# Eight memory recalls of a fused attention and GLU kernel: one float32 product each, replaced by three products of split operands

## The chip, the cores and the metric

The kernel runs on one core of one Trainium2 chip. The metric is the device time of one execution in microseconds (us); lower is better. Before the change the median of three runs is 689.55 us (689.37 to 689.55).

## The reference, cut to what matters

One layer with a residual: a layernorm, then two branches that both read it, and their sum.

```python
xn = layernorm(x)                        # 2048 tokens x 448
return x + A(xn) + B(xn)
# B: (sigmoid(xn @ w_gate) * (xn @ w_up)) @ w_down,   1792 hidden columns
# A: 16 heads of 28, the tokens in N = 4 blocks of L = 512, each block with causal attention of its own
M = z = 0
for s in range(N):
    a_dot = softmax(qs @ ks.T * scale + mask) @ vs
    pq = phi(qs)                         # t + 1 if t > 0 else exp(t)
    a_mem = (pq @ M) / (pq @ z + 1e-6)   # the recall: what earlier blocks left in the memory
    outs.append(g * a_mem + (1 - g) * a_dot)
    pk = phi(ks)
    M = M + pk.T @ vs;  z = z + pk.sum(tokens)
```

The line that the change touches is `pq @ M`, for the blocks s = 1, 2 (block 0 recalls an empty memory, and block 3 stays as it was).

## The kernel before

Most products run in float32r (f32r), which keeps fewer bits than float32. To keep float32 precision the kernel splits an operand in two f32r parts: a high part (a copy, ScalarE, line 85 or 436) and a low part (the operand minus its high part, VectorE or GpSimd, lines 86 and 437), and sums high x high, high x low and low x high in PSUM.

The program has a front and a long second stage. The front (lines 276 to 577) makes values, keys and queries of the four blocks of 512 tokens and keeps the memory; the second stage interleaves the GLU with the attention of the heads and ends with the output projection. The order of TensorE, ScalarE and VectorE in the front is the order in which the Python code is written; that of GpSimd is chosen by the scheduler. In each block b of the front:

- four times `values(b, t)`: 11 products of 128 x 448 (tile `pv`), and a copy on ScalarE that stores them in `vst`;
- between them, for b > 1, the recalls of block b - 1. A recall covers four heads (one of NG = 4 groups): it multiplies the group's memory `mst` (112 x 128, the four heads' blocks on a diagonal) with the features `phi` (112 x 512) that a DMA brought back from DRAM (`fd`). Recall i stands one call of `values` behind the one of its own number; recall 3 stands behind the first product of the next part;
- behind the product (tile `n`) VectorE transposes (line 402), divides and gates in `weigh` (lines 132, 133, 136), transposes back (line 404, tile `tb`), and GpSimd issues a DMA to `od` (line 405);
- seven times `keys_queries(b, c)`: 11 products of 128 x 512 (tile `pp`), whose split result goes to DRAM, and behind them the transposes of keys, `update(b, i)`, which adds to the memory (lines 389 and 390: VectorE, `dm` and `mst`), and `turn`, which transposes the next block's normalised tokens `xn` (tile `pt`, line 95).

In block 2, between the values, VectorE also takes the statistics of block 3's tokens (lines 294 to 296, ending in `vh`), and ScalarE takes their root `y` (line 301). That root stands in ScalarE's order in front of the copy of the second `values`. Block 3 has no statistics; in its place the split of a GLU weight, `wgu` (lines 85 and 86), stands there.

The 4k buffers (`four_k`, four of them) are shared by the split keys and queries and, from the change on, by what it adds.

Of the kernel before, what the change touches and what calls it, by code (L numbers as in the profile page):

```python
# [9 lines left out]
F32 = mybir.dt.float32  # L10
F32R = mybir.dt.float32r
AF = mybir.ActivationFunctionType
# [4 lines left out]
P = 128  # L17
# [10 lines left out]
NG = H // HG  # L28
GW = HG * DH
# [32 lines left out]
def kernel(  # L62
# [11 lines left out]
    V, A, G, T = nc.vector, nc.scalar, nc.gpsimd, nc.tensor  # L74
# [40 lines left out]
    def bank(name, tag):  # L115
        return ps.tile([P, L], F32, name=name, tag=tag, bufs=banks[tag])
# [10 lines left out]
    def weigh(pool, num, g, add):  # L127

        r = pool.tile([P, 16], F32, name="rc", bufs=2)
        n3 = num.rearrange("p (m c) -> p m c", c=32)  # L130
        if add:
            V.tensor_scalar_add(r, n3[:, :, DH], add)
            V.reciprocal(r, r)
        else:
            V.reciprocal(r, n3[:, :, DH])
        V.scalar_tensor_tensor(n3[:, :, :DH], n3[:, :, :DH], g, r.unsqueeze(2).to_broadcast([P, 16, DH]),
                               op0=ALU.mult, op1=ALU.mult)
# [11 lines left out]
    def four_k(dtype, name):  # L149
        return mid.tile([P, 2, L], dtype, name=name, tag="4k", bufs=4)  # L150
# [125 lines left out]
    with tc.tile_pool(name="front", bufs=2) as sb, tc.manual_schedule(engines=FRONT):  # L276
# [4 lines left out]
        wv = [late_pair("wv") for _ in range(4)]  # L281
        wv = [wv[c // 2][:, c % 2, :] for c in range(8)]
        wqk = [sb.tile([P, 8, P], F32R, name=f"wqk{c}", bufs=1) for c in range(7)]
        mst = [[sb.tile([GW, P], F32, name=f"mst{n}_{i}", bufs=1) for i in range(NG)] for n in range(2)]
        one = sb.tile([P, 1], F32, name="one", bufs=1)
        kn = eight_k(F32, "kn").rearrange("p (t a) n -> p t (a n)", t=NT)

        def statistics(b, t0, steps):

            stats = sb.tile([P, steps, 6], F32, name=f"stats{steps}")  # L290
            mv = sb.tile([P, steps, 2], F32, name=f"mv{steps}")
            vh = sb.tile([P, steps], F32, name=f"vh{steps}")
            for t in range(steps):
                V.bn_stats(stats[:, t, :], acc[b][:, t0 + t, :])
                V.bn_aggr(mv[:, t, :], stats[:, t, :])
            V.tensor_scalar(vh, mv[:, :, 1], EPS, -0.5, op0=ALU.add, op1=ALU.mult)
            return mv, vh

        def root(vh):
            y = sb.tile([P, vh.shape[1]], F32, name=f"y{vh.shape[1]}")  # L300
            A.activation(y, vh, AF.Sqrt, scale=-2.0)
            return y

        def rstd(mv, vh, y):

            steps = vh.shape[1]
            tm = sb.tile([P, steps], F32, name=f"tm{steps}")
            V.reciprocal(y, y)
            if steps == 1:
                V.tensor_scalar(tm, y, y, vh, op0=ALU.mult, op1=ALU.mult)  # L310
                V.tensor_scalar(y, tm, 1.5, y, op0=ALU.add, op1=ALU.mult)
            else:
                V.tensor_mul(tm, y, y)
                V.tensor_mul(tm, tm, vh)
                V.scalar_tensor_tensor(y, tm, 1.5, y, op0=ALU.add, op1=ALU.mult)
            return [(mv[:, t, 0:1], y[:, t:t + 1]) for t in range(steps)]

        def normalise(b, t, mean, y):
            xn = sb.tile([P, 512], F32, name="xn")
            V.tensor_scalar(xn[:, :D].rearrange("p (m h c) -> p h m c", h=H, c=4),  # L320
                              acc[b][:, t, :].rearrange("p (h m c) -> p h m c", h=H, c=4), mean, y,
                              op0=ALU.subtract, op1=ALU.mult)
            if b == 0:
                A.activation(xn[:, D:], xn[:, 384:D], AF.Copy)
            else:
                G.tensor_copy(xn[:, D:], xn[:, 384:D])
            return xn
# [15 lines left out]
        def values(b, t):  # L343
            pv = bank("pv", "p")
            value_terms(b, t, pv, EARLY[1] if b == 0 else TERMS)
            store_values(b, t, pv)
# [45 lines left out]
        def phi_queries(b, i):  # L392
            phi = sb.tile([GW, L], F32, name="phi", tag="e", bufs=5)
            nc.sync.dma_start(phi, fd[b][i * GW:(i + 1) * GW])
            return phi

        def recall(b, i, phi):
            ts = sb.tile([P, L], F32, name="ts", bufs=1)
            tb = sb.tile([P, L], F32, name="tb", bufs=2)
            n2 = bank("n2", ("m", "pd")[i % 2])  # L400
            T.matmul(n2, mst[b % 2][i], phi, start=True, stop=True)  # L401
            V.transpose(ts, n2)
            weigh(sb, ts, gate[:, i:i + 1], MEM_EPS)
            V.transpose(tb, ts)
            nc.gpsimd.dma_start(od[b][P * i:P * (i + 1)], tb)
# [28 lines left out]
        def split_qk(c):  # L434
            r = raw_qk[c].rearrange("p (c n) -> p c n", c=4)
            A.activation(wqk[c][:, 0:4, :], r, AF.Copy)
            G.tensor_sub(wqk[c][:, 4:8, :], r, wqk[c][:, 0:4, :].bitcast(F32))
# [66 lines left out]
        for b in range(NB):  # L504
            last = b == NB - 1
            phi, xn = {}, {}
            if b > 1:
                phi = {i: phi_queries(b - 1, i) for i in range(NG)}
            st = None
            for t in range(3 if b == 0 else 0, NT):  # L510
                values(b, t)
                if b > 1 and t > 0:
                    recall(b - 1, t - 1, phi[t - 1])
                if b == 0:
                    split_qk(t)
                if last:
                    continue
                if t == (3 if b == 0 else 0):
                    mv, vh = statistics(b + 1, 0, NT)
                if t == (3 if b == 0 else 0):  # L520
                    st = mv, vh, root(vh)
                if t == (3 if b == 0 else 2):
                    A.activation(one, ident[:, 0:1], AF.Exp)
            if st and b > 0:
                st = rstd(*st)
                for n in range(2):
                    xn[n] = normalise(b + 1, n, *st[n])
            e = {}
            for k, c in enumerate((3, 4, 5, 6, 0, 1, 2) if last else range(7)):
                e[c] = keys_queries(b, c)  # L530
                if b == 0 and c + 4 < 7:
                    split_qk(c + 4)
                if k == 0:
                    if b > 1:
                        recall(b - 1, NG - 1, phi[NG - 1])
                    if b == 0:
                        st = rstd(*st)
                    if b == 0:
                        A.activation(gate, gate, AF.Exp, scale=-1.0)
                        V.tensor_scalar_add(gate, gate, 1.0)  # L540
                        V.reciprocal(gate, gate)
                        V.tensor_scalar(gate_n, gate, -1.0, 1.0, op0=ALU.mult, op1=ALU.add)
                if (b, k) in ((0, 3), (1, 0)):
                    with tc.issue_after(stored[b, c]):
                        nc.sync.dma_start(acc[b + 2], x_block(b + 2))
                if (b, k) in ((2, 1), (3, 0)):
                    with tc.issue_after(stored[b, c]):
                        next(ffn)
                if last:
                    if k > 0:  # L550
                        next(ffn)
                    if 2 <= k < 6:
                        phi[k - 2] = phi_queries(b, k - 2)
                    if k > 4:
                        begin[k - 5]()
                        recall(b, k - 5, phi[k - 5])
                    continue
                if 2 <= k < 6:
                    key_rows(k - 2, e[k - 2])
                if 4 <= k:  # L560
                    update(b, k - 4)
                if k == 6:
                    update(b, 3)
                n = k - 1 if b == 0 else k + 1
                if 2 <= n < 6:
                    turn(b + 1, n - 2, xn[n - 2])
                if 0 <= n < 4 and n not in xn:
                    xn[n] = normalise(b + 1, n, *st[n])
                if b == 2 and k == 6:
                    next(ffn)  # L570
            if last:
                for i in range(2):
                    for _ in range(FILLS[i]):
                        next(ffn)
                    if i == 0:
                        begin[2]()
                    recall(b, i + 2, phi[i + 2])
# [3 lines left out]
    sb = ctx.enter_context(tc.tile_pool(name="att", bufs=1, reuse_waits="tile"))  # L581
# [252 lines left out]
```

## Time and profile before

| | before |
|---|---|
| median of three runs | 689.55 us |
| the profiled execution's own time | 689.46 us |
| its span in the trace | 687.7 us |
| granted clock of TensorE | 0.999 |
| TensorE / VectorE / ScalarE / GpSimd busy | 99% / 83% / 50% / 22% |
| products of recalls (line 401) | 24 instructions for 12 recalls, from 82.3 to 156.7 us |

The span is what the profiler recorded from the first to the last instruction; 1.76 us lie outside it. A row of a timeline has the start, the duration, the engine, the line, the operation, what it writes and reads, how many instructions are merged in it, and in brackets the idle time before it with what ended it. A row of the chain of waits has the start, the duration, the engine, the tile and the line. PE is TensorE, DVE VectorE, ACT ScalarE, POOL GpSimd. Types are printed as f32 in most rows whether the operand is float32 or f32r.

### The profile page before, as it was taken

The page shows a single profiled execution, that of the slowest core. Times are in us where ns is not written, and L with a number is a line of the kernel's source. Part 1 is how long each engine was busy: PE and PEld are TensorE (multiplying, and loading weights), DVE is VectorE, ACT ScalarE, POOL GpSimd, SP SyncE. Part 2 cuts the span into 40 slices and gives each one's busy share as a digit, 9 for nine tenths or more (in the row PEclk, how much of TensorE's full clock was granted, in tenths as well). Part 3 has the DMA queues.
Part 4 walks back from the last instruction along what each step waited for, and adds up shares of the span by engine and source line. Part 5 has one row for each costly group of instructions (what it writes and reads, how often), then busy time and mean ns, then how long its engine had stood idle before and what let it go on. Part 6 is the DMA issues. An engine that isn't in the chain of part 4 may idle for free.

```text
span 687.7 us, 10438 instructions
## 1 busy us (share of the span) xinstructions
PE 681.7 (99%) x3594; PEld 566.6 (82%) x3594; DVE 567.4 (83%) x994; ACT 342.6 (50%) x563; POOL 151.3 (22%) x349
## 2 busy tenths in 40 slices
PE   8999999999999999999999999999999999999997
PEld 7898888778878787787878878787787878878897
DVE  6765795767788988998898989989898899889863
ACT  4837555343554555543655446454653565446320
POOL 3500020101223222232332222322322322222000
PEclk9999999999999999999999999999999999999999
DMA  7446556696233323243223252314333332423342
GB/s 267 181 150 238 198 214 242 249 330 174 71 94 92 80 86 86 56 128 112 56 64 107 57 141 56 109 47 116 82 94 77 96 71 64 95 79 95 95 153 106
DMA packets 45796, 84.37 MB, mean 123 GB/s; under 512 B 6320, under 2 KB 20400, under 8 KB 45232
## 3 DMA queue, kind: packets, MB, share of 16 engines
q1 hardware_dynamic: 42736, 76.37, 35.8%
q0 software_dynamic: 3008, 7.34, 4.9%
q8 instruction: 28, 0.46, 0.3%
q14 instruction: 24, 0.20, 0.1%
HBM read 51.05 MB, written 32.64 MB: 122 GB/s over the span
## 4 chain that ended last, share of the span: by engine, by line
PE 70%; DVE 14%; issue 9%; POOL 4%; DMA 1%; ACT 1%; SPq 0%; POOLq 0%; ACTq 0%
PE pgu L247 26%; PE pd L173 13%; PE pp L355 10%; PE po L771 5%; PE pv L335 5%; PE st L612 3%; PE pa L687 3%; DVE mx L629 3%; DVE w L666 2%; POOL w L627 2%; DVE acc L174 2%; PE pmm L383 2%; PE n L401 2%; DVE hh L259 1%; DVE mx L633 1%
## 5 line engine op out<-in xcount | busy, mean ns | idle before, releaser
L247 PE MATMUL pgu<-xs,wgu 128*128 128x512 f32 x1232 | 304.1, 394 | 0.0
L247 PEld LDWEIGHTS pgu<-xs,wgu 128*128 128x128 f32 x1232 | 228.2, 188 | 47.4 <-issue 2.2
L173 PE MATMUL pd<-wdn,hh 128*128 128x448 f32 x672 | 156.0, 367 | 0.0
L627 POOL TENSOR_SCALAR_AFFINE_SELECT w<-w 128x256 f32<-128x256 f32 (+1 forms) x160 | 81.2, 509 | 236.4 <-ACT w L616 183.6
L173 PEld LDWEIGHTS pd<-wdn,hh 128*128 128x128 f32 x672 | 122.5, 188 | 12.3 <-issue 0.6
L667 ACT ACTIVATE w<-w 128x1024 f32<-128x1024 f32 (+1 forms) x96 | 87.3, 915 | 65.0 <-DVE w L666 64.2
L666 DVE TENSOR_TENSOR w<-w,mb 128x1024 f32<-128x1024 f32 (+1 forms) x96 | 98.9, 1045 | 0.1
L616 ACT ACTIVATE w<-st 128x512 f32<-128x512 f32 x128 | 74.9, 590 | 45.3 <-PE st L612 44.9
L629 DVE TRANSPOSE_TENSOR_REDUCE mx<-w 128x32 f32<-128x1024 f32 x64 | 79.0, 1235 | 17.0 <-POOL w L627 17.0
L355 PE MATMUL pp<-xs,wqk 128*128 128x512 f32 x308 | 77.7, 401 | 0.0
L174 DVE TENSOR_TENSOR acc<-pd,acc 128x448 f32<-128x448 f32 x112 | 67.1, 599 | 1.2 <-PE pd L173 1.1
L355 PEld LDWEIGHTS pp<-xs,wqk 128*128 128x128 f32 x308 | 56.8, 188 | 13.4 <-issue 2.4
L258 ACT ACTIVATE hh<-sg 128x512 fp32r<-128x512 f32 x56 | 35.2, 628 | 56.4 <-DVE sg L256 49.3
L612 PE MATMUL st<-qk 84*128 84x128 f32 (+3 forms) x256 | 61.9, 312 | 0.0
L255 ACT ACTIVATE sg<-pgu 128x512 f32<-128x512 f32 x56 | 33.2, 594 | 49.4 <-PE pgu L247 49.2
L612 PEld LDWEIGHTS st<-qk 84*128 84x128 f32 x256 | 47.6, 189 | 6.9 <-ACT w L616 0.3
L656 DVE STREAM_TRANSPOSE mb<-top 128x1024 f32<-128x1024 f32 x32 | 39.8, 1242 | 10.5 <-POOL top L653 10.1
L362 DVE TENSOR_TENSOR qk<-pp,qk 128x512 fp32r<-128x512 f32 x28 | 19.3, 688 | 29.8 <-ACT e L360 23.7
L259 DVE SCALAR_TENSOR_TENSOR hh<-sg,hh 128x512 fp32r<-128x512 f32 x56 | 38.7, 691 | 2.6 <-ACT hh L258 2.4
L335 PE MATMUL pv<-wv,xs 128*128 128x448 f32 x176 | 39.6, 376 | 0.4 <-DVE xs L102 0.3
L687 PE MATMUL pa<-w,vv 128*32 128x128 f32 (+3 forms) x512 | 39.7, 436 | 0.2
L256 DVE SCALAR_TENSOR_TENSOR sg<-sg,pgu 128x512 f32<-128x512 f32 x56 | 37.3, 665 | 1.8 <-PE pgu L247 1.6
(100 smaller groups left out, 640.6 us busy)
## 6 DMA issues: line engine op xcount, KB each, us to landing
qk<-qd SPq DMA_DIRECT2D x192, 112.0 KB
qd<-qk SPq DMA_DIRECT2D x28, 512.0 KB
raw<-in_w_ffn SPq DMA_DIRECT2D x14, 512.0 KB
vd<-vst SPq DMA_DIRECT2D x4, 1024.0 KB
vv<-vd SPq DMA_DIRECT2D x16, 256.0 KB
od<-w POOLq DMA_DIRECT2D x16, 256.0 KB, 3.8
sums<-od SPq DMA_DIRECT2D x32, 128.0 KB
out<-acc SPq DMA_DIRECT2D x16, 224.0 KB
```

What stands on the lines that cost most here:

```text
L173: T.matmul(pd[:, :D], l, r, start=n == 0, stop=n == len(mms) - 1)
L174: V.tensor_add(acc[b][:, t, :], pd[:, :D], acc[b][:, t, :])
L247: T.matmul(dst, wgu[f][:, w, side * P:(side + 1) * P], xs[b][:, a, :], start=n == 0, stop=n == len(TERMS) - 1)
L335: T.matmul(pv[:, :D], xs[b][:, a, t * P:(t + 1) * P], wv[w], start=n == 0, stop=n == len(TERMS) - 1)
L355: T.matmul(pp, wqk[c][:, w, :], xs[b][:, a, :], start=n == 0, stop=n == len(TERMS) - 1)
L612: T.matmul(st[:, at:at + L - kb * P], self.qk[:KS, 1, h, kb * P:(kb + 1) * P], self.qk[:KS, 0, h, kb * P:], start=True, stop=True)
L616: A.activation(w, st, AF.Copy)
L627: G.affine_select(d, d, pattern=pattern, base=0, channel_multiplier=-1, compare_op=ALU.is_ge, fill=MASK)
L629: V.tensor_reduce(mx[:, 16 * (n - 1):16 * (n + 1)], w3[:, n // 2, :2 * L].rearrange("p (b n) -> p b n", n=32), axis=mybir.AxisListType.X, ...
L666: V.tensor_sub(w, w, m)
L667: A.activation(w, w, AF.Exp, scale=SCALE)
L687: T.matmul(pa[32 * j:32 * j + 32, kb * P:], self.vv[:, kb, 32 * j:32 * j + 32], self.pairs[j // 2].block(j % 2, kb), start=kb == 0, stop=k ...
```

## The change

The eight recalls of blocks 1 and 2 (which run in blocks 2 and 3 of the front) become three f32r products each. The four memories of a block lie in one tile, so that one copy and one subtraction split all four (`memory_parts`, at the start of the block). Each recall's features are split by `parts`: for the first recall at the start of the block, for recall t between `values(b, t)` and recall t - 1. The high parts are copied on ScalarE, the low parts subtracted on GpSimd. The four recalls at the end of the front still are float32 products.

```diff
-        mst = [[sb.tile([GW, P], F32, name=f"mst{n}_{i}", bufs=1) for i in range(NG)] for n in range(2)]
+        memory = [sb.tile([GW, NG, P], F32, name=f"mst{n}", bufs=1) for n in range(2)]
+        mst = [[m[:, i, :] for i in range(NG)] for m in memory]
...
+        def memory_parts(b):
+
+            m = four_k(F32R, "ms")[:GW].rearrange("p a (i n) -> p a i n", i=NG)
+            A.activation(m[:, 0], memory[b % 2], AF.Copy)
+            G.tensor_sub(m[:, 1], memory[b % 2], m[:, 0].bitcast(F32))
+            return m
+
+        def parts(i, phi, m):
+
+            f = four_k(F32R, "phis")[:GW]
+            A.activation(f[:, 0, :], phi, AF.Copy)
+            G.tensor_sub(f[:, 1, :], phi, f[:, 0, :].bitcast(F32))
+            return [(m[:, a, i, :], f[:, w, :]) for a, w in ((0, 0), (0, 1), (1, 0))]
+
...
-            T.matmul(n2, mst[b % 2][i], phi, start=True, stop=True)
+            terms = phi if isinstance(phi, list) else [(mst[b % 2][i], phi)]
+            for n, (l, r) in enumerate(terms):
+                T.matmul(n2, l, r, start=n == 0, stop=n == len(terms) - 1)
...
                 phi = {i: phi_queries(b - 1, i) for i in range(NG)}
+                mp = memory_parts(b - 1)
+                phi[0] = parts(0, phi[0], mp)
...
                 if b > 1 and t > 0:
+                    phi[t] = parts(t, phi[t], mp)
                     recall(b - 1, t - 1, phi[t - 1])
```

ScalarE at the start of block 2, before: the last exponential of block 1's features (`e`), the copies of the values (`vst`) and the root `y` between the first and the second.

```order
L361 ACTIVATE e<-e 128x512
L339 ACTIVATE vst<-pv 128x16x28
L301 ACT_TABLE_LOAD
L301 ACTIVATE y_936<-vh_926 128x4
L339 ACTIVATE vst<-pv 128x16x28 x2
```

The same place now:

```order
L362 ACTIVATE e<-e 128x512
L401 ACTIVATE ms<-mst_123 112x512
L408 ACTIVATE phis<-phi 112x512
L340 ACTIVATE vst<-pv 128x16x28
L302 ACT_TABLE_LOAD
L302 ACTIVATE y_936<-vh_926 128x4
L340 ACTIVATE vst<-pv 128x16x28
L408 ACTIVATE phis<-phi 112x512
L340 ACTIVATE vst<-pv 128x16x28
L408 ACTIVATE phis<-phi 112x512
```

The copies of the memory (`ms`) and of the first features stand ahead of the first `vst`; the copy of the second recall's features stands behind the root and behind the second `vst`.

GpSimd in block 2 before: nothing but the DMAs of the recalls' results and the copies of a strip of `xn`.

```order
L326 COPY xn<-xn 128x64 x7
L405 DMA od_92<-tb 128x512 x3
L326 COPY xn<-xn 128x64 x2
L405 DMA od_92<-tb 128x512
L326 COPY xn<-xn 128x64 x2
```

GpSimd in block 2 now:

```order
L327 COPY xn<-xn 128x64 x7
L402 TENSOR_TENSOR ms<-mst_123,ms 112x512
L409 TENSOR_TENSOR phis<-phi,phis 112x512 x2
L422 DMA od_92<-tb 128x512
L409 TENSOR_TENSOR phis<-phi,phis 112x512
L422 DMA od_92<-tb 128x512
```

Three subtractions stand ahead of the first DMA; that of the third recall's features stands behind the DMA of the first recall's result, and that of the fourth behind the DMA of the second. VectorE's and the DMA queue's orders are the same as before.

## The prediction

> **What bounds the kernel now.** I read the page first, then the chain of waits in the stretch where the recalls run, then the timelines of that stretch.
>
> ```profile
> PE 681.7 (99%) x3594; PEld 566.6 (82%) x3594; DVE 567.4 (83%) x994; ACT 342.6 (50%) x563; POOL 151.3 (22%) x349
> ```
>
> A busy share of 99% is an average over stages, so the stage decides. The chain of waits through block 2 of the front:
>
> ```profile
> 78.06 4.42 PE pv L335 x22
> 82.48 0.86 PE n L401 x2
> 83.34 2.21 PE pv L335 x11
> 85.55 0.86 PE n L401 x2
> 86.41 2.21 PE pv L335 x11
> 88.61 0.86 PE n L401 x2
> 89.47 2.51 PE pp L355 x11
> 91.99 0.86 PE n L401 x2
> 92.85 2.52 PE pp L355 x11
> 95.37 0.44 PE pt L95 x4
> ...
> 119.42 0.86 PE n L401 x2
> ```
>
> Each piece begins where the one before ends: TensorE sets the pace here without a gap, so TensorE time saved in a recall is time saved, and any wait put into TensorE's order is time lost. Both pass in full to what follows, since TensorE works through its order strictly in sequence.
>
> **What is removed.** A float32 recall costs 0.86 us on the chain. An f32r product of the same 512 columns costs 2.51 / 11 = 0.228 us (the pp piece), so three cost 0.685. Each recall gains 0.175 us, eight gain 1.40 us. That is the whole gain; the transposes, gates and DMAs behind a recall stay.
>
> **What is added, and on whose time.** Two times five copies on ScalarE and two times five subtractions on GpSimd. The nearest rows are the split of a query weight in the first block, which has the same 512 columns:
>
> ```profile
> L437 POOL TENSOR_TENSOR wqk<-stage,wqk 128x512 fp32r<-128x512 f32 x4 | 5.1, 1293 | 4.8 <-ACT wqk L436 4.8
> ...
> L436 ACT ACTIVATE wqk<-stage 128x512 fp32r<-128x512 f32 x4 | 2.4, 621 | 0.0
> ```
>
> I take 1.29 us for a subtraction and 0.62 for a copy: 12.9 us more on GpSimd and 6.2 on ScalarE, neither on the chain by itself. In such a row the busy time and the mean of one in ns stand behind the first bar.
>
> Here a rule can be held against the row. The Trainium skill, GPSIMD Engine Reference, section 3.1 (Elementwise), gives a two-input GpSimd operation about 2.6 cycles an element; at the 1.2 GHz that it uses, an estimate by that page is 1.11 us for 512 columns. With it the three subtractions ahead of the second recall would be done 0.55 us sooner, and the sum below would end near +1.4 instead of +2.0 us. The row was measured in this kernel, and it decides.
>
> **What GpSimd's subtractions do to VectorE.** This is the step on which the forecast rests. First the rows:
>
> ```profile
> 18.95 3.79 POOL L437 TENSOR_TENSOR wqk<-stage,wqk 128x512 fp32r<-128x512 f32 x3 [1.10 <-ACT wqk L436]
> 19.11 0.59 DVE L294 BATCH_NORM_STATS2 stats<-acc 128x6 f32<-128x448 f32 x1
> ...
> 25.55 1.30 POOL L437 TENSOR_TENSOR wqk<-wqk_raw,wqk 128x512 fp32r<-128x512 f32 x1 [2.81 <-ACT wqk L436]
> 25.80 1.08 DVE L313 TENSOR_TENSOR tm<-y 128x4 f32<-128x4 f32 x1
> 26.91 0.16 DVE L314 TENSOR_TENSOR tm<-tm,vh 128x4 f32<-128x4 f32 x1
> ...
> 486.99 1.21 DVE L86 TENSOR_TENSOR wgu<-raw,wgu 128x1024 fp32r<-128x1024 f32 x1
> 487.12 1.75 POOL L652 COPY top<-top 32x32 f32<-32x32 f32 x1 [0.28 <-DVE top L651]
> 488.12 0.67 DVE L259 SCALAR_TENSOR_TENSOR hh<-sg,hh 128x512 fp32r<-128x512 f32 x1
> ```
>
> While GpSimd subtracts, VectorE's statistics (one input from SBUF) take their usual 0.59 us. But the 128x4 product at 25.80, with two inputs from SBUF, takes 1.08 us where its like a moment later takes 0.16, and it ends at 26.88, just behind the subtraction's end at 26.85: it was held until GpSimd was done. The other way round a tiny GpSimd copy at 487.12 lasts 1.75 us, until two back-to-back VectorE operations of that kind are over (488.79). So I read: a VectorE operation with two SBUF inputs and a GpSimd operation exclude each other; whichever is second waits for the end of the first.
>
> **Block 2, step by step.** The rows of the place where the new work lands:
>
> ```profile
> 75.51 0.46 SPq L394 DMA_DIRECT2D phi<-fd  x1
> 77.47 0.63 ACT L361 ACTIVATE e<-e 128x512 f32<-128x512 f32 x1
> 79.06 0.29 DVE L390 TENSOR_TENSOR mst<-mst,dm 112x128 f32<-112x128 f32 x1
> 79.58 0.29 DVE L390 TENSOR_TENSOR mst<-mst,dm 112x128 f32<-112x128 f32 x1
> 79.79 0.62 DVE L294 BATCH_NORM_STATS2 stats<-acc 128x6 f32<-128x448 f32 x1
> 82.85 0.17 DVE L296 TENSOR_SCALAR vh<-mv 128x4 f32<-128x4 f32 x1
> 83.05 0.20 ACT L301 ACTIVATE y<-vh 128x4 f32<-128x4 f32 x1 [0.89 <-DVE vh L296]
> 83.16 0.53 ACT L339 ACTIVATE vst<-pv 128x448 f32<-128x448 f32 x1
> 83.38 0.72 DVE L402 STREAM_TRANSPOSE ts<-n 128x512 f32<-128x512 f32 x1 [0.36 <-PE n L401]
> 84.63 0.68 DVE L136 SCALAR_TENSOR_TENSOR ts<-ts,gate,rc 128x448 f32<-128x448 f32 x1
> 85.35 0.71 DVE L404 STREAM_TRANSPOSE tb<-ts 128x512 f32<-128x512 f32 x1
> 86.38 0.76 POOL L405 DMA_DIRECT2D od<-tb  x1 [20.41 <-DVE tb L404]
> ...
> 91.48 0.71 DVE L404 STREAM_TRANSPOSE tb<-ts 128x512 f32<-128x512 f32 x1
> 92.95 0.93 DVE L320 TENSOR_SCALAR xn<-acc,mv,y 128x448 f32<-128x448 f32 x2
> ```
>
> ScalarE is free at 78.10, behind `e`. It copies the memory until 78.72 and the first features until 79.34, if these have landed (issued until 75.97; the trace has no landing time, only that TensorE read them at 82.48). GpSimd then subtracts from 78.72 to 80.01 and from 80.01 to 81.30. The first recall, at 82.48, finds both ready: no wait there.
>
> VectorE, however, wants its two memory updates (`mst`, two SBUF inputs) at 79.06 and 79.58. The first is held to 80.01; `dm` between them brings the second to about 80.4, inside the second subtraction, and it is held to 81.30. The statistics then begin at about 81.35 instead of 79.79, and all that hangs on them comes 1.56 us later: `vh` ends at 84.58, the root `y` at 84.81, and the second `vst`, behind it on ScalarE, at 85.25. Only then comes the copy of the second recall's features, to 85.87, and its subtraction, to 87.16. Without the hold it would have ended near 85.60.
>
> The second recall begins at 85.55 - 0.175 = 85.37. Its first product needs only high parts; the second product is due at 85.60 and waits until 87.16. The recall ends two products later, at 87.62, where the float32 one ended at 86.41: 1.21 us behind, 0.35 of gains already counted. Behind it on TensorE stand the fourth `pv` and everything else.
>
> What comes next depends on a near tie. VectorE's first transpose now begins at 84.58, and its gate (line 136, two SBUF inputs) 1.25 us later, at 85.83, against the subtraction at 85.87.
>
> - *GpSimd first*: the gate is held to 87.16, `tb` ends at 88.55, the DMA is issued at 88.87 (0.32 behind, as before) and takes until 89.6, and only behind it GpSimd subtracts for the third recall, to 90.9. That recall's second product is due at 87.62 + 2.21 + 0.23 = 90.06: 0.85 us of waiting. In the same way the fourth (due 94.10, ready 94.45) waits 0.35. With a short wait for `xn`, which also comes later, `pt` starts at 97.5 instead of 95.37: +2.1 us.
> - *VectorE first*: the subtraction ends at 87.80 and the second recall waits 2.2 us, but later ones find theirs ready; the fourth ends near 94.35 instead of 92.85: +1.5 us.
>
> I take +1.8 for block 2, gains included.
>
> **Block 3.** Here there is no root, and a weight's split stands at the start:
>
> ```profile
> 114.94 1.04 ACT L85 ACTIVATE wgu<-raw 128x1024 fp32r<-128x1024 f32 x1
> 116.52 0.29 DVE L390 TENSOR_TENSOR mst<-mst,dm 112x128 f32<-112x128 f32 x1
> 116.73 1.22 DVE L86 TENSOR_TENSOR wgu<-raw,wgu 128x1024 fp32r<-128x1024 f32 x1
> ```
>
> In times of before (block 2's loss shifts all alike), the memory's copy ends at 116.6, and GpSimd meets VectorE's `mst` and, back to back with it, the 1.22 us of `wgu`. Held until 117.95, GpSimd ends its two subtractions at 120.54; the first recall's second product is due at 119.65. It waits 0.9 us, and the three later recalls then find theirs ready: net 0.9 - 0.70 = +0.2. If GpSimd gets in first and keeps the turn, nothing waits: about -0.6. I take +0.2, since two of the three orders of the tie lead there.
>
> **The sum.** +1.8 + 0.2 = +2.0 us on the profiled execution's 689.46 gives 691.46; the median stands 0.09 above that execution, so 691.5 us. The second stage begins later by that much and has no gap in TensorE's chain at its start in which to give it back.
>
> **The rivals.**
>
> - *No wait at all* (not slower). If neither engine holds the other for long and each subtraction fits, only the gain is left: 689.55 - 1.40 = 688.1. It decides at the second recall: its low part must be there at 85.60, and without any hold it ends at about 85.6, with nothing to spare. Against it is the row at 25.80. 0.13.
> - *Half of it.* If the first features land only after about 79.7, their subtraction starts behind the second `mst`, and only the first is held: the statistics shift by 0.8, the second recall waits 0.8, the later ones hardly. Block 2 ends at +0.1, and block 3 without its wait at -0.6: 689.0. The trace does not exclude so late a landing. 0.20.
> - *VectorE does not recover.* It is some 3.5 us behind when block 2's keys begin, and the transposes of `xn` (`pt`) and the keys' features hang on it. If one or two `pt` wait as well, another 1 to 1.5 us go: 692.5 to 693. Against it: after 104 us VectorE had idle time before each product. 0.12.
>
> **How the numbers follow.** The forecast has 0.55; its own range, with the ties both ways, is 1.5 - 0.6 = +0.9 to 2.1 + 0.25 + 0.3 (small further waits) = +2.65: 690.4 to 692.2. The range of 688.6 to 692.8 takes in the half case and the milder end of the last one, and leaves out the case without waits (0.13) and the worst of the last (0.05). A measurement of this kernel can tell about 0.2%, 1.38 us, from no change. Faster by more: half of the no-wait case, 0.07, since its 1.40 lies on that bound. Same: the other half, the half case and the low end of the forecast, 0.33. Slower: 0.60.
>
> **What would show it.** Right: the recall's pieces on the chain reading near 0.69 without waits; the second product of the second recall waiting over a microsecond for GpSimd; the two `mst` before block 2's statistics lasting 0.9 us instead of 0.29; `vh` ending 1.5 us later. Wrong: `mst` at 0.29 with GpSimd subtracting beside it, subtractions far from 1.29 us, or a `pv` behind the second recall that starts before 85.6.

## The result, and the profile after

The changed kernel takes 693.56 us (median of 5 runs, 692.00 to 694.12), the kernel before in the same set 689.52 (689.37 to 689.55). The ratio is 1.0052, 95% interval 1.0039 to 1.0064: slower, by 4.0 us at the medians. The forecast was 691.5 in a range of 688.6 to 692.8. The five runs lie in two groups: 692.00 and 692.09, and 693.56, 693.62 and 694.12. The profiled one is that of 692.00 us, with a span of 690.3 against 687.7, so its trace shows 2.6 us of the loss; the rest shows only in other runs.

The page's line of busy times, after:

```profile
PE 680.9 (99%) x3602; PEld 567.0 (82%) x3602; DVE 573.2 (83%) x994; ACT 347.6 (50%) x573; POOL 166.7 (24%) x359
```

TensorE is busy 0.8 us less than before. GpSimd has the ten subtractions more (15.4 us), ScalarE the ten copies (5.0). VectorE has 5.8 us more with the same 994 instructions: nothing was given to it, so it was held. The rows of single lines of code say where (minimum, median and maximum in ns):

```profile
L391 DVE TENSOR_TENSOR mst<-mst,dm x8: 291/293/1090, 70.8 to 118.2; 112x128 f32<-112x128 f32 x8
L132 DVE TENSOR_SCALAR rc<-ts x12: 159/178/1395, 85.1 to 166.8; 128x16 f32<-128x16 f32 x12
```

Before, the maxima of these two were 294 and 180 ns. The first was forecast; the second, an addition to 16 columns with one tensor as its input, was not. Block 2 in the timeline of the changed kernel:

```profile
78.56 1.30 POOL L402 TENSOR_TENSOR ms<-mst,ms 112x512 fp32r<-112x512 f32 x1 [12.73 <-ACT ms L401]
78.92 1.09 DVE L391 TENSOR_TENSOR mst<-mst,dm 112x128 f32<-112x128 f32 x1
79.82 1.34 POOL L409 TENSOR_TENSOR phis<-phi,phis 112x512 fp32r<-112x512 f32 x1
80.25 1.07 DVE L391 TENSOR_TENSOR mst<-mst,dm 112x128 f32<-112x128 f32 x1
84.28 0.17 DVE L297 TENSOR_SCALAR vh<-mv 128x4 f32<-128x4 f32 x1
85.02 0.62 ACT L408 ACTIVATE phis<-phi 112x512 fp32r<-112x512 f32 x1
85.60 0.69 DVE L136 SCALAR_TENSOR_TENSOR ts<-ts,gate,rc 128x448 f32<-128x448 f32 x1
85.69 0.50 PE L418 MATMUL n<-phis,ms 112*128 112x512 f32 x1 [0.44 <-ACT phis L408]
85.72 1.70 POOL L409 TENSOR_TENSOR phis<-phi,phis 112x512 fp32r<-112x512 f32 x1 [4.56 <-ACT phis L408]
87.47 0.74 PE L418 MATMUL n<-phis,ms 112*128 112x512 f32 x2 [1.27 <-POOL phis L409]
92.10 1.40 DVE L132 TENSOR_SCALAR rc<-ts 128x16 f32<-128x16 f32 x1
92.15 1.30 POOL L409 TENSOR_TENSOR phis<-phi,phis 112x512 fp32r<-112x512 f32 x1
```

Each `mst` ends just behind the subtraction beside it (80.01 and 79.86, 81.32 and 81.16). `vh` comes at 84.28 instead of 82.85, the copy of the second recall's features (85.02) behind it. VectorE won the near tie at the gate (85.60 against 85.72), GpSimd's subtraction was stretched to 1.70, and the second recall waited twice: its first product 0.44 us for the copy of the high part, the two others 1.27 us for the subtraction. At 92.10 the small addition lasts until 93.50, just behind the end (93.45) of the subtraction that began 0.05 us later.

Block 3, the same view:

```profile
118.26 2.51 POOL L402 TENSOR_TENSOR ms<-mst,ms 112x512 fp32r<-112x512 f32 x1 [12.03 <-ACT ms L401]
118.40 1.22 DVE L86 TENSOR_TENSOR wgu<-raw,wgu 128x1024 fp32r<-128x1024 f32 x1
122.06 0.73 PE L418 MATMUL n<-phis,ms 112*128 112x512 f32 x2 [0.74 <-POOL phis L409]
126.49 1.25 DVE L132 TENSOR_SCALAR rc<-ts 128x16 f32<-128x16 f32 x1
130.34 1.35 DVE L132 TENSOR_SCALAR rc<-ts 128x16 f32<-128x16 f32 x1
131.71 0.73 PE L418 MATMUL n<-phis,ms 112*128 112x512 f32 x2 [0.33 <-POOL phis L409]
```

And TensorE's chain:

```profile
93.68 0.69 PE n L418 x3
94.37 2.50 PE pp L356 x11
96.88 0.54 PE pt L95 x4
...
116.66 4.43 PE pv L336 x22
...
159.33 6.60 PE pgu L247 x29
```

Here `pgu` is the second stage's product with a GLU weight; further down, `st` is the product that gives the attention's scores, `pd` that with a down weight, and `pa` that of the attention's weights with the values. `wgu` and `wdn` are the split GLU and down weights. A recall without waits takes 0.69 us, as forecast (0.685). `pt` stood at 95.37 before (+1.51 here), the `pv` of block 3 at 115.00 (+1.66), the first long `pgu` at 156.68 (+2.65). So in this run block 2 lost 1.66 us and block 3 about 1.0, gains counted in, and nothing was lost behind.

### The profile page after: what moved, and what is told of

It is laid out like the page before. It is cut to its first block, busy times and chain, and to the rows that moved or that the text cites. A ratio compares the mean times of both kernels' runs of the same rounds, so it can differ in the third digit from the quotient of the medians.

```text
span 690.3 us, 10489 instructions
## 1 busy us (share of the span) xinstructions
PE 680.9 (99%) x3602; PEld 567.0 (82%) x3602; DVE 573.2 (83%) x994; ACT 347.6 (50%) x573; POOL 166.7 (24%) x359
## 4 chain that ended last, share of the span: by engine, by line
PE 69%; DVE 14%; issue 9%; POOL 5%; ACT 1%; DMA 0%; POOLq 0%; ACTq 0%
PE pgu L247 27%; PE pd L173 13%; PE pp L356 10%; PE po L791 5%; PE pa L707 4%; PE st L632 4%; PE pv L336 3%; DVE mx L649 2%; POOL w L647 2%; DVE w L686 2%; DVE acc L174 1%; PE pmm L384 1%; DVE mx L653 1%; DVE hh L259 1%; PE n L418 1%
## 5 line engine op out<-in xcount | busy, mean ns | idle before, releaser
L356 PE MATMUL pp<-xs,wqk 128*128 128x512 f32 x308 | 76.1, 396 | 0.0
L336 PE MATMUL pv<-wv,xs 128*128 128x448 f32 x176 | 38.1, 367 | 0.3 <-POOL wv L449 0.2
```

The lines of the kernel that those rows point to most:

```text
L336: T.matmul(pv[:, :D], xs[b][:, a, t * P:(t + 1) * P], wv[w], start=n == 0, stop=n == len(TERMS) - 1)
L356: T.matmul(pp, wqk[c][:, w, :], xs[b][:, a, :], start=n == 0, stop=n == len(TERMS) - 1)
```

## Experiments

### What the change gains, and what the subtractions cost

**e1: no low parts.** The ten subtractions are left out; three products of the high parts are added, so the recall leaves out what the low parts give.

```diff
-            G.tensor_sub(f[:, 1, :], phi, f[:, 0, :].bitcast(F32))
-            return [(m[:, a, i, :], f[:, w, :]) for a, w in ((0, 0), (0, 1), (1, 0))]
+            return [(m[:, 0, i, :], f[:, 0, :])] * 3
```

> Leaves out the ten GpSimd subtractions; each of the eight recalls still has three f32r products, all of high parts. Theory (what costs is waiting for the low parts, through VectorE and GpSimd holding each other up): only the gain of 8 x 0.175 us is left, 689.5 - 1.4 = 688.1 us, no wait of a recall for GpSimd, block 2's statistics end where they did before (vh at about 83.0). Rival (the ScalarE copies and the 4k buffers cost, or three products gain less than 0.175 us): 689 us or more.

Measured: 688.17 us (10 runs, 688.09 to 688.38), ratio 0.9982, interval 0.9973 to 0.9992. That is 1.25 us below the kernel before, where the sum of the gains said 1.40; in its trace the first long `pgu` starts 1.41 us earlier (155.27 instead of 156.68). `mst` is back at 291 to 294 ns. The gain is real; the subtractions eat it and more. The ten copies and the buffers, which e1 keeps, cost next to nothing.

**e8: one product instead of three.** As e1, with a single product of high parts.

> Leaves out the low parts and two of the three products: one f32r product of high parts for each of the eight recalls, so the recalled values keep only f32r precision. No GpSimd subtraction, no hold. TensorE saves 8 x (0.86 - 0.23) = 5.06 us. Theory: in block 2 VectorE had only 1.4 us to spare between xn and its transposes, so 2.5 us saved on TensorE do not all pass: 685.5 to 687.5 us, with pt waiting for xn. Rival (TensorE sets the pace whatever else): 684.4 us.

Measured: 684.52 us (4 runs, 684.45 to 684.94), ratio 0.993, interval 0.9916 to 0.9945. A recall takes 0.24 us on the chain. The theory (685.5 to 687.5, part of it lost at `xn`) missed, and the rival came. Between e1 and e8 sixteen products of 0.228 us are gone, 3.65 us, and the time fell by 3.65. TensorE's time in a recall passes through in full. This version is faster than both kernels, but its recall has only the precision of one f32r product.

### Is it the wait for the low parts?

**e2: dead parts.** The copies and subtractions stay and nobody reads them; the recalls are float32 as before.

```diff
-            return [(m[:, a, i, :], f[:, w, :]) for a, w in ((0, 0), (0, 1), (1, 0))]
+            return phi
```

> All copies and subtractions stay, but nothing reads them: the recalls are the single float32 products of before. Theory: VectorE is held as in the changed kernel (the memory updates before the statistics 1.1 us instead of 0.29, vh 1.4 us late), but TensorE does not wait for GpSimd, and what VectorE is late is hidden: 689.3 to 690.0 us. Rival (the holds of VectorE and the extra copies cost TensorE time by themselves, through late xn and late buffers): 691 us or more.

Measured: 693.96 us (4 runs, 693.46 to 694.67), ratio 1.0067, interval 1.0052 to 1.0082. The theory, that TensorE's wait for low parts is the whole loss, gave at most 690 and fell. The timeline of e2:

```profile
79.09 1.09 DVE L391 TENSOR_TENSOR mst<-mst,dm 112x128 f32<-112x128 f32 x1
80.41 1.07 DVE L391 TENSOR_TENSOR mst<-mst,dm 112x128 f32<-112x128 f32 x1
88.05 1.61 DVE L132 TENSOR_SCALAR rc<-ts 128x16 f32<-128x16 f32 x1
92.27 1.40 DVE L132 TENSOR_SCALAR rc<-ts 128x16 f32<-128x16 f32 x1
96.75 0.85 PE L95 MATMUL pt<-ident,xn 128*128 128x128 f32 x4 [1.35 <-DVE xn L321]
172.06 0.50 PE L632 MATMUL st<-qk 84*128 84x512 f32 x1 [1.48 <-ACT w L636]
```

In block 2 VectorE is held four times; it comes to `xn` late, and TensorE waits for `xn` instead. So in block 2 the wait for low parts in the changed kernel hides this one: VectorE's lateness is the cause, and TensorE pays it at one door or the other. That is not all of e2, though. Against the kernel before, its chain is 1.83 us late at block 3's `pv` (116.83) and still 1.82 late behind block 3's recalls (131.61 against 129.79): where nobody waits for low parts, block 3 loses nothing, so the 1.0 us that the changed kernel loses there is the wait for low parts itself. The other 3.0 us of e2 come behind the front (the first `pa` at 207.98 instead of 203.12), among them the 1.48 us of the last row; the last section of experiments is about these.

**e3: features two recalls ahead.**

```diff
+                if b > 1:
+                    if t + 1 < NG:
+                        phi[t + 1] = parts(t + 1, phi[t + 1], mp)
...
-                    phi[t] = parts(t, phi[t], mp)
```

> Each recall's features are split one call of values earlier, so that the second recall's copy stands ahead of the root on ScalarE and each subtraction ahead of the DMA that it stood behind on GpSimd. Theory: the wait of the second recall in block 2 (1.5 us) and the wait of the fourth in block 3 (0.4) go, the first recall's wait in block 3 (1.0) stays: 689.1 us, within 688.7 to 689.8. Rival (the subtractions are late because GpSimd is slow or the features land late, whatever the order): the waits move to other recalls, 691 us or more.

Measured: 693.54 us (4 runs, 692.80 to 693.78), ratio 1.0058, interval 1.0043 to 1.0073: a miss. The timeline:

```profile
88.00 2.79 DVE L132 TENSOR_SCALAR rc<-ts 128x16 f32<-128x16 f32 x1
88.23 2.52 POOL L409 TENSOR_TENSOR phis<-phi,phis 112x512 fp32r<-112x512 f32 x2
89.57 0.73 PE L418 MATMUL n<-phis,ms 112*128 112x512 f32 x2 [1.10 <-POOL phis L409]
96.66 0.84 PE L95 MATMUL pt<-ident,xn 128*128 128x128 f32 x4 [0.64 <-DVE xn L321]
```

The second recall no longer waits; the third does, behind a pair of subtractions, and `xn` is late as well. The addition at 88.00 was held through both subtractions: VectorE didn't get its turn between them. TensorE's first `pgu` is 2.09 us late here (134.24 against 132.15) where the changed kernel's is 2.65 late, so something was gained in the front; 1.8 us more are lost behind it (the first `pa` at 206.99).

**e7: subtractions on VectorE.** `V.tensor_sub` for `G.tensor_sub` in both places.

> The ten subtractions run on VectorE (about 0.6 us each) instead of GpSimd. Theory (VectorE's time between its memory updates and xn is what is short in block 2; holds and work there cost alike): five subtractions add about 3 us to VectorE where the holds added 3.1, so block 2 ends about as late as in the changed kernel: 691 to 693.5 us. Rival (a GpSimd subtraction is slow and queues behind DMAs, and only that costs): 690 us or less.

Measured: 691.3 us (6 runs, 690.34 to 692.54), ratio 1.0026, interval 1.0014 to 1.0039, in the expected range. Its `mst` take 0.29 us; VectorE is not held, it simply has more to do, and TensorE waits 0.59 us for `xn` at `pt`. The first `pgu` is 0.75 us late (132.90), and another 1.05 are lost behind the front (`pa` at 204.92). It is 2.3 us better than GpSimd, on the busier engine.

### Block 3, and a split that doesn't collide

**e6: memory split a block earlier, features two ahead**, in both blocks.

```diff
-                mp = memory_parts(b - 1)
...
+                if b in (1, 2) and k == 3:
+                    mp = memory_parts(b)
```

> The memory is split in the block before, beside VectorE work with PSUM inputs, and the features two calls ahead. Theory: of VectorE's holds in block 2 one memory update (0.8) and one or two later ones (1.2) remain instead of 4.3 us in all, the recalls of block 3 do not wait: block 2 ends +0.6, block 3 -0.7, together 689.0 to 690.5 us. Rival (the holds are not what costs, since the amount of GpSimd work is the same): 692 us or more, as in the changed kernel.

Measured: 691.72 us (10 runs, 690.37 to 692.95), ratio 1.0032, interval 1.0022 to 1.0041. Block 3's recalls take 0.86 to 0.87 us in the timeline, where pipelined matmuls overlap, without a wait; block 2's third still waits 1.04 and `pt` 0.64. The best runs are in the expected range, the median isn't.

**e10: only block 3's four recalls changed**, split as in e6.

```diff
+                if last:
+                    phi[0] = parts(0, phi[0], mp)
...
+                if b == 2 and k == 3:
+                    mp = memory_parts(b)
```

> Only block 3's four recalls as three f32r products (memory split a block earlier, features two calls ahead), block 2's four stay float32: five copies and five subtractions instead of ten each. Theory: block 2 is as in the kernel before (pt at 95.4 less a tenth), block 3's recalls find their parts ready and save 4 x 0.175 = 0.70 us, VectorE's held operations there cost TensorE at most 0.3: 688.8 to 689.2 if block 3's stores start within 0.5 us of where they did (130.8), and 689.2 to 690.3 if VectorE brings them 1 us or more later and weights land late. Rival: the subtractions' collisions in block 3 alone cost as much as the changed kernel lost there, 690.5 or more.

Measured: 689.51 us (10 runs, 688.72 to 693.81), ratio 1.001, interval 0.9995 to 1.0026: no difference, and a miss, above the 688.8 to 689.2 that the theory gave for stores that start in time. All four recalls run without a wait on the chain (0.69 to 0.71 us), and block 3's first store of keys is issued at 130.73 against 130.80 before. Yet the profiled run is 690.50 us: the 0.7 us gained is lost again behind the front, where a weight's split waited 2.86 us for its load and TensorE 1.48 us for an `st`.

### What the other 1.5 us are

**e4: the changed kernel again.**

> The changed kernel once more, for its two levels (692.0 and 693.6 us in its first five runs). Theory: the levels come from a near tie of VectorE and GpSimd in blocks 2 and 3; a run of the upper level shows TensorE's recalls 1.5 us later by the end of the front than the first profile (159.3 us), and the same second stage. Rival: the front is the same in both levels and the second stage differs.

Measured: 693.74 us (4 runs, 693.41 to 694.38). This time the profile is one of the upper group (693.63). The theory missed and the rival came: its front is that of the run above (the fourth recall at 131.78 against 131.71), the second stage isn't. The chain of waits:

```profile
152.37 7.56 DMA raw<-in_w_ffn
...
160.02 1.07 ACT wgu L85
...
170.83 0.59 ACT w L636
...
171.46 0.51 PE st L632
```

and the rows of the waiting engines:

```profile
160.02 1.06 ACT L85 ACTIVATE wgu<-raw 128x1024 fp32r<-128x1024 f32 x1 [2.45 <-DMA raw<-in_w_ffn]
161.11 1.22 DVE L86 TENSOR_TENSOR wgu<-raw,wgu 128x1024 fp32r<-128x1024 f32 x1 [3.44 <-ACT wgu L85]
171.46 0.51 PE L632 MATMUL st<-qk 84*128 84x512 f32 x1 [1.25 <-ACT w L636]
```

The load of the third weight took 7.56 us. Its split stands in ScalarE's and VectorE's order among the last recalls, so both engines stood behind it, and TensorE waited 1.25 us for an `st`. Before, this split started at 153.90 after a wait of 0.38; in the run of 692.00 at 158.32 after 0.90.

In these traces a late weight costs nothing by itself. What counts is where the split starts against TensorE's first long `pgu`. Before, it starts 2.22 us ahead of it (153.90 against 156.12 in the timeline); in the run of 692.00 only 0.45 ahead (158.32 against 158.77), since the load was issued 3.85 us later than before (152.66 against 148.81) and took 0.6 longer, while TensorE was only 2.65 late; in e4 it starts 1.21 behind. Twelve traces have the split at this place in the order of the engines. In the five in which it starts ahead (before, after, e1, e6 and e8, by 0.30 to 2.22 us) TensorE does not wait for that `st`; in the seven in which it starts behind (e2, e3, e4, e7, e10, e11 and e12, by 0.23 to 2.68) it waits 0.55 to 1.48 us.

**e5: that split queued behind the first gated products.**

```diff
+                        if f0 == 0 and (b, slot) == (1, 2):
+                            with tc.issue_after(act.ins), tc.issue_after(dve.ins):
+                                ahead[b, slot]()
```

> The changed kernel, with one step of the second stage queued later: the split of the third GLU weight (wgu) stands on ScalarE and VectorE behind the second stage's first gated products instead of between the last recalls. Theory: the upper level of the changed kernel comes from that split, whose weight lands late (at 160.0 instead of 158.3 us) because the DMA engines start block 3's stores late and are full until 165 us; the split holds ScalarE and VectorE while it waits. With it out of the way every run is at the lower level, 691.7 to 692.3 us. Rival (the late loads hold the first attention scores, or the second stage is late for another reason): the upper level stays, median 693.5 us.

Measured: 692.03, 692.17, 693.49 and 693.98 us, ratio 1.0051, interval 1.0036 to 1.0066. Both groups are still there: a miss. The profile is that of 692.17, of the lower group: the split of a down weight waited 2.74 us for its load in it, and TensorE waited for nothing behind the front. What held the two upper runs no trace shows.

**e9: without block 3's stores.** The seven stores of block 3's split keys and queries are left out; its attention reads block 2's.

> The changed kernel without block 3's stores of split keys and queries (seven transfers of 512 KB left out; block 3's attention reads block 2's instead), all instructions of TensorE, VectorE, ScalarE and GpSimd unchanged. Theory: the second part of the loss, about 1.6 us in most runs, is weights that land late because the DMA engines run full from 135 to 165 us with those stores in front; without them the split of wgu finds its weight landed (waits below 0.5 us) and all runs lie at 691.5 to 692.2, within 0.5 us of each other, with the recalls' waits for low parts and the late xn as they were (pt at 96.9). Rival: the late landing is not from these stores; the median stays at 693.3 to 693.9 and the weights' splits still wait 2 us or more for DMA.

Measured: 699.41 us (4 runs, 697.43 to 700.87), ratio 1.0141, interval 1.0119 to 1.0164: a miss that says nothing on its question, since the program's order moved. ScalarE and VectorE got the third weight's split several places earlier, ahead of the copy of the last keys (`qk`):

```profile
157.91 1.06 ACT L85 ACTIVATE wgu<-raw 128x1024 fp32r<-128x1024 f32 x1 [8.34 <-DMA qk<-qd]
```

```profile
150.00:165.00 15.00, 10.71 (x35) 6.89 (x34) 8.02 (x15) 4.07 (x7) 0.54 (x1) 0.87 0.80 233
```

ScalarE stood 8.34 us in front of it, TensorE was busy 10.71 of 15 us, and its granted clock (the third number from the end) fell to 0.87 on the mean of the stretch, 0.58 from 160 to 166 us. It does show what a split queued ahead of its load can cost.

**e11: the load earlier.** The third weight's load moves from SP's queue to GpSimd's, which is idle there; ScalarE's order is held by hand.

```diff
-                nc.sync.dma_start(raw_up[f], w_ffn[f][:, :1024])
+                (nc.gpsimd if f == 2 else nc.sync).dma_start(raw_up[f], w_ffn[f][:, :1024])
```

> The changed kernel with one load moved: the third weight of the second stage (512 KB) is issued on GpSimd's queue, which is idle there, instead of on SP's behind the keys' and features' transfers; ScalarE's order is held as it was. Nothing of the front changes, so its loss stays (first pt near 96.9, recalls waiting as before). Theory: the load is issued near 148 us, when its buffer comes free, instead of 152.4, so it lands by about 156 and ScalarE's split of it no longer waits; the upper level goes away and all runs lie at 691.6 to 692.3. Rival: the upper level comes from somewhere else in the DMA-full stretch (the last features, the down weight, the attention's twelve loads); the median stays at 693.2 to 693.9.

Measured: 694.02 us (4 runs, 692.80 to 694.62), ratio 1.0064, interval 1.0047 to 1.0081: a miss. The load was issued at 148.17 instead of 152.37 and its split no longer waited; the down weight behind it did:

```profile
159.33 0.58 ACT L86 ACTIVATE wdn<-rawd 128x448 fp32r<-128x448 f32 x1 [3.52 <-DMA rawd<-in_w_ffn]
```

Against 1.23 us in e4. TensorE waited 0.47 us for the last features, which it did not before, and 0.55 for `st`. The trace gives the DMA engines a busy share of 0.93 and 1.02, that is full, in the two stretches of 5 us from 150 to 160: here what one transfer gained others lost.

**e12: the same load moved, on e10.**

> The same moved load in the kernel that has only block 3's recalls as three products. Theory: its run of 688.7 is the one in which no weight is late, and the others (to 693.8) are late loads; with the load earlier the median is 688.6 to 689.0 with all runs below 689.6. Rival: the spread is not from this load; the median stays near 689.5, with single runs above 691.

Measured: 690.30 us (10 runs, 689.16 to 691.77), ratio 1.0012, interval 1.0003 to 1.0022: a miss, in part for the same reason: in the profiled run (691.40) the down weight's split waited 4.03 us instead of 1.09, TensorE 0.82 for the last features and 0.72 for `st`. Another 0.56 us had been lost before the change had any part in it (`pt` at 95.72 against 95.16 in e10).

**e13 and e14: the two loads left out.** The third weight's splits read weights that are already there, so no load can be late; every engine's order is held, but for one swap of neighbours on VectorE. e13 is the changed kernel, e14 the one before, as the control.

```diff
+            if f == 2:
+                raw_up[2] = raw_up[1]
+                return
...
+            if f == 2:
+                raw_down[2] = raw_down[0]
+                return
```

> The changed kernel without the two loads of the second stage's third weight (its two splits read the weights already there; 740 KB less on the DMA engines at 150 to 160 us; the order of every engine as it was, but for one swap of neighbours on VectorE). Theory: all that the changed kernel loses behind the front is these splits' waiting for late weights, so the loss of the front alone is left, 2.65 us on a control that lies at 689.1 to 689.5: 691.6 to 692.2 in every run, all within 0.5 us, first pa near 205.7. Rival: there is another cause behind the front (the attention's loads, the clock, later collisions): 693.2 or more, or runs over 1 us apart.

> The control: the kernel before without the same two loads. Both theories: its splits waited 0.38 us at most, beside VectorE work, so 689.1 to 689.5 as before; if it is faster than 689.0, its weights were late too, and the difference to the run above is to be taken from here.

Measured: e13 692.34, 692.37, 692.42, 693.61 and 693.61 us; e14 689.69 (10 runs, 689.52 to 689.90); the ratios to the kernel before are 1.0045, interval 1.0031 to 1.0059, and 1.0002, interval 0.9993 to 1.0012. The three runs at 692.4 lie 2.7 us above the control, as the theory said, though both stand some 0.2 us above their expected ranges: with no late weight the front's loss alone is left. The two at 693.61 are against it, and the profile is one of them. No split waits for a load there. Its chain:

```profile
85.76 1.71 POOL phis L423
87.47 0.04 issue
87.51 0.72 PE n L432 x2
88.24 3.72 PE pv L350 x11
91.95 0.77 PE n L432 x3
```

The `pv` behind the second recall takes 3.72 us instead of 2.22, with nothing to wait for. The stretches of the trace show the clock (third number from the end):

```profile
84.00:88.00 4.00, 2.28 (x10) 1.50 (x9) 2.87 (x8) 3.44 (x7) 2.24 (x2) 1.00 0.01 2
88.00:92.00 4.00, 4.00 (x14) 3.57 (x13) 2.87 (x5) 0.16 (x2) 1.88 (x3) 0.57 0.19 70
92.00:96.00 4.00, 4.00 (x18) 3.26 (x18) 3.10 (x5) 1.73 (x4) 1.45 (x2) 1.00 0.81 328
```

Behind the wait for low parts, in four microseconds of which TensorE was busy 2.28, the granted clock went to half for about 3 us (0.78, 0.50, 0.50 and 0.51 in the microseconds from 88 to 92). That run took 1.2 us more than its fellows. The same pause stands in five other traces (the changed kernel at 692.00, e4, e5, e9 and e11: TensorE busy 2.28 or 2.29 us from 84 to 88), and there the clock stayed at 1.00 until 92: the pause alone does not bring it down. Both runs at 693.61 have a mean granted clock of 0.998, the three at 692.4 one of 1.000, and 0.002 of 690 us is 1.4 us. So there are two causes of some 1.5 us each, either of which puts a run into the upper group: late weights (e4's profile, clock 0.999) and a clock that drops behind the wait (e13's). Of the changed kernel's first five runs those of 693.56 and 693.62 us have 0.998 and fit the second, that of 694.12 has 0.999 and fits the first, and the two at 692.0 have 1.000; only the last kind is backed by a trace of that set, so the assignment of the others is an inference. The two slowest runs of e10, 692.58 and 693.81 us, have 0.998 too, though no recall waits in e10's trace, so a drop at that pause is not the only one there can be. What decides in which runs the clock drops, and why the same load takes 5.7 us in one run and 7.6 in another, stays open.

## Why the prediction was wrong

- **The gain: right.** 1.40 us by rows, 1.41 on e1's chain and 1.25 in its time, 0.69 us for a recall.
- **The mechanism and block 2: right in kind and size.** VectorE's `mst` held to the end of a subtraction, `vh` 1.4 us later, the copy and the subtraction of the second features behind it, over a microsecond of waiting at the second recall: all seen. +1.8 was forecast, the mean of two branches; +1.66 was measured. The near tie went to VectorE, and that branch said +1.5 with the fourth recall's end near 94.35: it ended at 94.37. One slip did no harm: the second recall's first product was to start at 85.37, while the copy that it reads was to end at 85.87; it started at 85.69, and the low part came later still. The price of 1.29 us for a subtraction held (1.28 to 1.34 where it was free); by the figure of the Trainium skill, GPSIMD Engine Reference, section 3.1, the sum would have been further off.
- **What was missed in it.** The prediction let only operations with two SBUF inputs be held. The addition of `rc` (L132) has one, 16 columns wide, and was held up to 1.40 us in the changed kernel and 2.79 in e3. The Trainium skill, SBUF — State Buffer, section "SBUF: two separate sides", says that a port pair which VectorE shares with GpSimd is locked for a whole instruction, and that VectorE takes part also with a one-input operation in a two-port mode. The rows of L132 fit this, though no row shows the mode that it ran in; the prediction had drawn the line from the statistics alone, which weren't held. This is why moving the parts (e3) does not cure it.
- **Block 3's term: too small.** +0.2 was forecast, about +1.0 measured. The first recall's wait came as worked out (0.9; measured 1.0 by where the recall ends, 0.74 as idle time in the row). "The three later recalls then find theirs ready" failed: two more additions were held, 1.25 and 1.35 us, VectorE came late to the transposes and the DMAs that stand ahead of the subtractions on GpSimd, and the fourth recall waited as well.
- **The step that failed outright: the sum stops at the end of the front.** "The second stage begins later by that much and has no gap in TensorE's chain at its start in which to give it back" hands the front's loss on unchanged and puts nothing for what may be lost on top. It held in the runs near 692.0 (+2.65 at `pgu`, +2.6 at the end). In the others, the median among them, 1.5 us come on top. In e4 the third weight's split, 2.2 us ahead of TensorE before the change, came 1.2 us behind it, and TensorE waited 1.25 us for `st`; in e13 the clock fell behind the pause at the second recall, and a `pv` took 3.72 us instead of 2.22. The prediction treated a wait as worth its own length, and the first stage's end as the end of its effects.
- **Why the weight was so late is shown only in part.** Block 3's stores start later (the first at 134.06 instead of 130.80), the load behind them is issued 3.6 to 3.9 us later, and this eats about 1 us of the 2.2. The rest is the load's own time, 5.1 us before and up to 7.6 here, and that does not hang on late stores: in e10 the first store is in time, the load is issued at 149.05 against 148.81 before, and still it took 7.8 us.
- **The rivals.** "VectorE does not recover" (0.12, 692.5 to 693) came nearest: e2, e3 and e7 show its waits for `xn`. In the changed kernel itself they are hidden behind the low parts' wait, and its number came near by another way, through the 1.5 us of the upper group. "Half of it" fell: the first features' subtraction ran at 79.82, and both `mst` were held. "No wait at all" (688.1) is e1's time.

With the measured sizes of both blocks the sum would have been 1.66 + 1.0 = 2.65, or 692.1: the lower group. Nothing in the profile of before has a row for the clock's drop. For the late weight it had a hint: a load of 5.1 us on DMA engines that were 0.96 to 0.97 busy from 150 to 160 us, and a split only 2.2 us ahead of TensorE.

## What to carry to other kernels

Work given to an idle GpSimd is paid by VectorE where the two meet: list VectorE's operations beside the new work, small ones too, and give those that can be held the rest of the subtraction beside them. Here additions on SBUF tensors (112x128 and 128x16) were held, and before the change a 128x4 product; the statistics (0.59 us) and the transpose from SBUF to SBUF (0.71) were not. Taking one wait out then moves the loss to the next door (low parts, `xn`, a weight); an experiment that keeps the work but lets nobody wait for it (e2) tells what is really late, and in which block. Before adding up, look behind the changed stretch as well: for each load that TensorE will need there, how far ahead of TensorE its split runs. Where little is left, or where a busy TensorE is made to pause, a delay can cost more than its length, and in some runs only.

## What the runs showed of the hardware

- Two subtractions queued back to back on GpSimd kept VectorE out for both: 2.79 us for an operation of 0.18 (e3). The other way round, `mst` and the split of `wgu` back to back stretched a subtraction of 1.29 to 2.51 us.
- TensorE's granted clock fell to 0.50 for about 3 us behind two waits of 0.44 and 1.28 us, in a stretch of 4 us with 2.28 busy (e13's trace; by their mean clock two of its five runs). Behind the same pause it stayed at 1.00 in five other traces. The Trainium skill, TensorE: Matmul & The Clock Gate, section "Part 1: The HAM clock gate (the "warmup" mystery)", knows the half clock and windows of 3.4 us, and lets it come after an idle window; here TensorE's idle time was about half of that, so a window that is only partly idle seems to be enough at times; no run settles it.
- The load of the third weight (512 KB) took 5.1 us before, 5.7 in the run of 692.00, 7.6 in e4 and 7.8 in e10, though in e10 it was issued within 0.3 us of its time before.
- Sixteen f32r products less (e8 against e1) brought 3.65 us, 0.228 each, the price read from the chain.
